# Queries and keys in 96 partitions of six tokens, and the order of the first loads, in a fused attention and expert kernel

## The chip, the cores and the metric

The kernel runs on one core of a Trainium2 chip. The metric is the device time of one execution in microseconds (us); of several executions, the median. The engines are TensorE (PE, with its weight loads as PEld), VectorE (DVE), ScalarE (ACT), GpSimd (POOL) and SyncE (SP), which issues most transfers. A transfer issued from SP, ScalarE or GpSimd stands in that engine's queue; an issue that waits holds up whatever is behind it.

## The reference

Causal attention for 4 batches of 8 heads, 576 tokens, head size 64, with a bias from running sums of a score per token, then a routed expert layer and a last feed-forward layer. Of it the change touches the attention:

```
scores = scale * q @ k.T                      # (4, 8, 576, 576)
cum = cumsum(maximum(s, 0))                   # s: (4, 8, 576)
bias = -(cum[:, :, :, None] - cum[:, :, None, :])
scores = where(causal, -1e9, scores + minimum(bias, 0))
attn = exp(scores - max(scores)); attn = attn / sum(attn)
out = attn @ v
```

## The kernel before, in words

The heads go in 8 groups g of four, each group in two pairs pr of heads. A float32 operand is held as two parts, a high one rounded to float32r and a low remainder, and products are summed over the parts. The order of work is written out in steps t: a prologue from t = -16 (PRE = 16), then 224 blocks of scores from t = 0, seven for each of 32 heads. At each step `todo[t]` runs first, then one block (`emit_s`, L943 on), then at most two jobs of a list sorted by due step (`run_job`). `later(n, ...)` puts work n steps on. So the order of instructions on each engine is fixed when the program is built.

Loading a pair of heads (`load_qk`, L700): queries and keys come as 128 tokens in partitions for four blocks of tokens, and the last 64 tokens in a transfer of their own. That makes 6 transfers for a pair, all on SP. `t_unit` (L802) transposes them on TensorE against an identity, so that a token becomes a column: 4 blocks of 128 for the queries, 4 for the keys, and 2 for the tails. ScalarE evicts the high part from PSUM (L821), VectorE subtracts for the low part (L826). `dup` (L837) copies or transfers the parts to the tiles QKA and QKB, from which the scores are made; for g = 0 and 1 a string of letters says which of the six moves goes to ScalarE (a), VectorE (v) or a transfer (d).

The bias goes in by extra rows of the score product. In QA (queries) and KA (keys) partitions 0 to 63 hold the head's values. Partitions 64 to 68 hold ones and bias rows: KA 64 and 65 hold the high and low part of the running sum, QA 66 and 67 the negated ones, QA 68 the negated row maximum; the rest are ones. The running sums are made once, at the start (L741 to L746): maximum, scan, high part, low part on VectorE, two negations on ScalarE, in four rows of `brow`. Group 0 takes its rows by four transfers on SP (L755 to L759); the other groups take theirs from a copy in DRAM, `b_dram` (L762, `bias_rows` L831).

`guard` (L886) makes the scores a first time to find each row's maximum; VectorE reduces them (L903) with a throwaway output `junk`. `m_row` (L913) transposes the maxima, and a transfer on SP (L927) places the negated maxima in QA 68. A block needs that transfer. `v_split` (L866) makes the high and low part of the values.

The constants of the start: `ident` on GpSimd, the rows of ones on VectorE and GpSimd (L730, for g = 1 at t = -9), `identb` as a VectorE copy of `ident` (L774), `band`, `tri` and others on GpSimd. The values of group 0 are loaded by SP from t = -8, the gate weights (`load_w`, L714) by SP at t = 6.

Of the kernel before, what the change touches and what calls it, by code (L numbers as in the profile page):

```python
# [8 lines left out]
F32 = mybir.dt.float32  # L9
# [19 lines left out]
def fb(ap):  # L29
    return ap.bitcast(F32)  # L30
# [136 lines left out]
def build(ctx, tc, q, k, v, s, w_gate, w1, w2, w_in, w_out, out, debug=None):  # L167
# [13 lines left out]

    b_dram = dram.tile([32, 4, S], F32, name="b_dram")
    K = {}
# [498 lines left out]
def attention(ctx, tc, const, cv, q, k, v, s, w_gate, ident, L, x_dram, b_dram, setup):  # L682
    nc = tc.nc
    NG = 2 * B
    NB, LAG, GLAG, PRE = 28, 5, 5, 16
    one = ctx.enter_context(tc.tile_pool(name="a_one", bufs=1))
# [4 lines left out]

    qkraw = [one.tile([128, 2, 5, 2, D], F32, name=f"qkraw{i}") for i in range(2)]
    vraw = one.tile([128, 5, 4, D], F32, name="vraw")
# [6 lines left out]
    def load_qk(g, pr, n):  # L700

        t, h, src = n % 2, n // 2, (q, k)[n % 2]
        h0 = 4 * (g % 2) + 2 * pr
        if h < 2:
            nc.sync.dma_start(out=qkraw[pr][:, t, 0:4, h],
                              in_=src[g // 2, h0 + h, 0:512].rearrange("(i p) d -> p i d", p=128))
        else:
            nc.sync.dma_start(out=qkraw[pr][:64, t, 4],
                              in_=src[g // 2, h0:h0 + 2, 512:S].rearrange("h p d -> p h d"))

# [15 lines left out]
    KB, QB = [x[:, :, :S] for x in QKB], [x[:, :, S:] for x in QKB]  # L726
    brow = QKB[1][:32].rearrange("p h c -> p (h c)")[:, :4 * S].rearrange("p (j c) -> p j c", j=4)

    def ones(i, engine, heads):
        engine.memset(fb(QKA[i])[64:69, heads], 1.0)  # L730

    def pads(i):
        nc.gpsimd.memset(fb(QA[i])[0:64, :, 0:64], 0.0)

    nc.vector.memset(spos, 0.0)
# [4 lines left out]
    pads(0)  # L740
    nc.vector.tensor_scalar(srow, srow, 0.0, 8.0, op0=OP.max, op1=OP.mult)  # L741
    nc.vector.tensor_tensor_scan(scan, srow, spos, 0.0, op0=OP.add, op1=OP.add)
    nc.vector.tensor_copy(brow[:, 2], scan)
    nc.scalar.activation(brow[:, 0], scan, AF.Copy, scale=-1.0)
    nc.vector.tensor_sub(brow[:, 3], scan, fb(brow)[:, 2])
    nc.scalar.activation(brow[:, 1], fb(brow)[:, 3], AF.Copy, scale=-1.0)  # L746

# [6 lines left out]

    for j in (2, 0, 3, 1):  # L755
        if j < 2:
            nc.sync.dma_start(out=fb(QA[0])[66 + j:67 + j, :, 64:], in_=fb(brow)[0:4, j])
        else:
            nc.sync.dma_start(out=fb(KA[0])[62 + j:63 + j], in_=fb(brow)[0:4, j])  # L759
    for n in range(6):  # L760
        load_qk(0, 1, n)
    nc.sync.dma_start(out=b_dram, in_=fb(brow))  # L762
    nc.gpsimd.memset(vraw[64:128, 4], 0.0)
# [4 lines left out]
    init_v(0)  # L768
    idwg = one.tile([128, 128 + 4 * E], F32, name="idwg")
    nc.gpsimd.tensor_copy(idwg[:, 16:144], ident)  # L770
    tiny = one.tile([128, 1], F32, name="tiny")
    nc.gpsimd.memset(tiny, 1e-9)
# [29 lines left out]
    def t_unit(g, pr, n):  # L802

        if n == 0:
            QK[g, pr] = rot.tile([128, 4, S], F32R, name="qk", bufs=2)
        st = QK[g, pr]
        p = bank()
        if n < 2:
            for r in range(4):
                nc.tensor.transpose(p[:, 128 * r:128 * r + 128], qkraw[pr][:, n, r], ident)  # L810
            src, hd = p, st[:, 1 + n, 0:512]
            los = [(src, hd, st[:, 3 * (1 - n), 0:512])]
        else:
            for t in range(2):
                nc.tensor.transpose(p[:, 128 * t:128 * t + 128], qkraw[pr][:, t, 4], ident)
            src = p[:, :256].rearrange("p (t c) -> p t c", t=2)[:, :, :64]
            hd = st[:, 1:3, 512:]
            los = [(src[:, t], st[:, 1 + t, 512:], st[:, 3 * (1 - t), 512:]) for t in range(2)]
# [12 lines left out]
    def bias_rows(g, pr):  # L831
        i, hs = g % 2, slice(2 * pr, 2 * pr + 2)
        rows = b_dram[4 * g + 2 * pr:4 * g + 2 * pr + 2].rearrange("h j t -> j h t")
        nc.sync.dma_start(out=fb(QA[i])[66:68, hs, 64:], in_=rows[0:2])
        nc.sync.dma_start(out=fb(KA[i])[64:66, hs], in_=rows[2:4])

    def dup(g, pr):  # L837
# [48 lines left out]
    def guard(g, pr, u):  # L886
# [186 lines left out]
    for g in range(NG):  # L1073
        s0 = NB * g
        for pr in range(2):
            b = s0 + 14 * pr
            for n in range(3):
                at = {0: -PRE + 9 * pr, 1: 4 + 6 * pr, 2: 16 + 6 * pr}.get(g, b - 52) + n
                job(at, max(at, b - 49 + 2 * n), t_unit, g, pr, n)
        pl = []  # L1080
        if g == 0:
            pl += [(8 - PRE + n // 2, load_v, (g, n)) for n in range(5)] + [(22 - PRE, load_w, ())]
        if g:
            for pr in range(2):
# [15 lines left out]
    while t < len(blocks) or queue or jobs or any(k >= t for k in todo):  # L1100
# [63 lines left out]
```

## Time and profile before

| | us |
|---|---|
| median of 3 runs | 1044.74 (1041.9 to 1045.15) |
| the profiled execution's own time | 1042.71 |
| its span, first to last instruction | 1041.0 |
| TensorE busy in the span | 956.0 (92%) |
| VectorE busy | 635.1 (61%) |
| ScalarE busy | 624.3 (60%) |
| GpSimd busy | 428.2 (41%) |

The times of instructions below count from the start of the span. Lines (L826) are those of the kernel before. The attention takes about the first 293 us of the span, the experts and the last layer the rest. The granted clock is a share of TensorE's full clock.

### The profile page before, as it was taken

The numbers are of one execution on the slowest core, as the hardware profiler recorded it, in microseconds if no ns is written. First come the engines' busy times: TensorE is split into PE (matmuls) and PEld (weight loads), VectorE is DVE, ScalarE is ACT, GpSimd is POOL, SyncE is SP. The second block draws the span as 40 slices with busy tenths as digits, with TensorE's granted clock in tenths as the row PEclk, the third lists the DMA queues.
The fourth block names the chain that finished last, engine by engine and source line by source line (L and its number), as shares of the span: only waits on it lengthen the run. The fifth ranks groups of instructions, "written<-read, shape, count | busy, mean of one in ns | idle before, by whom it ended". The sixth has DMA issues, their size and how long they took to land.

```text
span 1041.0 us, 21440 instructions
## 1 busy us (share of the span) xinstructions
PE 956.0 (92%) x7695; PEld 922.6 (89%) x7695; DVE 635.1 (61%) x1893; ACT 624.3 (60%) x1389; POOL 428.2 (41%) x425
## 2 busy tenths in 40 slices
PE   6979989999936779899999999999999999999996
PEld 5879878988836679899999999999999999999996
DVE  7667797798676668655545644644655564443243
ACT  4657776676842346645745664674674575675574
POOL 5446666467766632460342125036035123602401
PEclk8789998899966889999999999999999999999998
DMA  5799989895237433330321212123123022501200
GB/s 120 177 191 204 209 185 208 198 211 133 64 105 221 144 104 90 97 105 2 94 75 41 71 51 89 42 65 105 40 65 93 13 84 69 150 12 30 76 2 23
DMA packets 133298, 105.57 MB, mean 101 GB/s; under 512 B 63720, under 2 KB 114056, under 8 KB 133160
## 3 DMA queue, kind: packets, MB, share of 16 engines
q1 hardware_dynamic: 122520, 83.50, 32.6%
q10 hardware_dynamic: 7600, 11.27, 3.6%
q0 software_dynamic: 3072, 9.44, 2.9%
q8 instruction: 60, 0.98, 0.4%
q14 instruction: 46, 0.38, 0.1%
HBM read 69.55 MB, written 9.73 MB: 76 GB/s over the span
## 4 chain that ended last, share of the span: by engine, by line
PE 60%; DVE 14%; issue 10%; DMA 6%; ACT 5%; POOL 3%; SPq 1%; ACTq 0%; POOLq 0%; DVEq 0%
PE y L472 8%; PE y L474 8%; PE y L473 8%; PE hp L472 5%; PE hp L474 5%; PE hp L473 5%; PE words L472 3%; PE words L474 3%; PE words L473 2%; DMA QKB<-qk 2%; PE rt L260 2%; DVE mask L256 2%; DVE junk L903 1%; PE pv L1002 1%; PE pv L1004 1%
## 5 line engine op out<-in xcount | busy, mean ns | idle before, releaser
L442 POOL TENSOR_TENSOR wt<-raw,wt 128x512 fp32r<-128x512 f32 x112 | 142.8, 1293 | 167.4 <-ACT wt L441 161.5
L982 POOL TENSOR_TENSOR Pl<-P,Ph 128x384 fp32r<-128x384 f32 (+2 forms) x128 | 136.4, 1073 | 97.0 <-DVE Ph L981 43.9
L472 PE MATMUL y<-act,WO 128*128 128x288 f32 x516 | 156.4, 303 | 0.0
L473 PE MATMUL y<-act,WO 128*128 128x288 f32 x516 | 153.5, 297 | 0.2
L474 PE MATMUL y<-act,WO 128*128 128x288 f32 x516 | 153.6, 298 | 0.0
L472 PE MATMUL hp<-xu,WI 128*128 128x288 f32 x372 | 113.4, 305 | 6.7 <-DVE c L574 5.4
L474 PE MATMUL hp<-xu,WI 128*128 128x288 f32 x372 | 111.0, 298 | 0.0
L473 PE MATMUL hp<-xu,WI 128*128 128x288 f32 x372 | 110.0, 296 | 0.0
L473 PEld LDWEIGHTS y<-act,WO 128*128 128x128 f32 x516 | 98.2, 190 | 0.6 <-DVE act L580 0.6
L474 PEld LDWEIGHTS y<-act,WO 128*128 128x128 f32 x516 | 98.6, 191 | 0.0
L472 PEld LDWEIGHTS y<-act,WO 128*128 128x128 f32 x516 | 98.5, 191 | 0.0
L377 POOL DMA_INDIRECT xg<-x_dram,idx x24 | 22.5, 939 | 184.2 <-DVE rt L383 178.9
L441 ACT ACTIVATE wt<-raw 128x512 fp32r<-128x512 f32 x112 | 70.0, 625 | 40.7 <-DMA raw<-in_moe_w_dram 12.9
L974 ACT ACTIVATE P<-s 128x384 f32<-128x384 f32 (+2 forms) x128 | 63.7, 503 | 40.3 <-PE s L967 24.3
L566 ACT ACTIVATE c<-c 128x288 f32<-128x288 f32 x128 | 56.5, 441 | 45.6 <-DVE c L565 41.7
L574 DVE SCALAR_TENSOR_TENSOR hp<-c,hp 128x288 f32<-128x288 f32 x75 | 34.5, 460 | 76.3 <-ACT c L569 76.1
L472 PEld LDWEIGHTS hp<-xu,WI 128*128 128x128 f32 x372 | 70.8, 190 | 9.3 <-DVE c L574 7.2
L1002 PE MATMUL pv<-Ph,VH 128*128 128x320 f32 (+4 forms) x224 | 74.0, 330 | 4.5 <-DVE xT L1021 4.2
L965 PE MATMUL s<-QKB 128*128 128x320 f32 (+4 forms) x224 | 71.6, 320 | 0.0
L473 PEld LDWEIGHTS hp<-xu,WI 128*128 128x128 f32 x372 | 71.0, 191 | 0.3
L474 PEld LDWEIGHTS hp<-xu,WI 128*128 128x128 f32 x372 | 70.9, 190 | 0.0
L1004 PE MATMUL pv<-Pl,VH 128*128 128x320 f32 (+4 forms) x224 | 68.2, 304 | 1.4 <-POOL Pl L982 1.3
(274 smaller groups left out, 2991.9 us busy)
## 6 DMA issues: line engine op xcount, KB each, us to landing
raw<-in_moe_w_dram SPq DMA_DIRECT2D x120, 256.0 KB
QKB<-qk SPq DMA_DIRECT2D x55, 288.0 KB
QKA<-qk SPq DMA_DIRECT2D x29, 288.0 KB
qkraw<-in_q_dram SPq DMA_DIRECT2D x32, 128.0 KB
qkraw<-in_k_dram SPq DMA_DIRECT2D x32, 128.0 KB
vraw<-in_v_dram SPq DMA_DIRECT2D x32, 128.0 KB
x_dram<-xn SPq DMA_DIRECT2D x16, 256.0 KB
r<-in_moe_w_in_dram ACTq DMA_DIRECT2D x8, 512.0 KB
```

The costliest lines, as they stand in the source:

```text
L441: nc.scalar.activation(t[:, 0], r, AF.Copy)
L442: nc.gpsimd.tensor_sub(t[:, 1], r, fb(t)[:, 0])
L472: nc.tensor.matmul(out_ap, ah, bh, start=first, stop=False)
L473: nc.tensor.matmul(out_ap, ah, bl, start=False, stop=False)
L474: nc.tensor.matmul(out_ap, al, bh, start=False, stop=last)
L566: nc.scalar.activation(a, a, AF.Exp)
L574: nc.vector.scalar_tensor_tensor(u, a, 0.5, p[:, :CAP], op0=OP.subtract, op1=OP.mult)
L965: nc.tensor.matmul(p[:m, at:at + n], KB[i][:, h, kc], QB[i][:, h, q0:q1], start=ti in (1, 2) and j == 0, stop=False, skip_group_check=True)
L974: nc.scalar.activation(P[:, :n], p[:, :n], AF.Exp, scale=0.125)
L982: nc.gpsimd.tensor_sub(Pl[:, :n], P[:, :n], fb(Ph)[:, :n])
L1002: nc.tensor.matmul(o, VH[i][:, a, hs], ph, start=first, stop=False)
L1004: nc.tensor.matmul(o, VH[i][:, a, hs], pl, start=False, stop=last)
```

## The change

Queries and keys are loaded as 96 partitions of six consecutive tokens (NR = 6, NP = 96): one transfer for each head of each of the two, 4 for a pair. A transpose takes 96 tokens, every sixth one, so ScalarE's eviction and VectorE's subtraction write the columns at a step of six words. Units 0 and 1 of a pair do five residues of queries or keys, unit 2 the last residue of both.

The rows of the running sum are no longer negated. QA's ones become plain ones and KA's rows 66 and 67 become -1 (`signs`, made on ScalarE for g = 0 and GpSimd for g = 1), so `brow` and `b_dram` hold two rows in place of four. Group 0's rows go by SP for QA and by ScalarE's queue for KA, after the evictions at t = -13.

The first loads, for both pairs and for the values of group 0, stand at the head of SP. `identb` is built by GpSimd, the ones of the first group by VectorE, those of the second by GpSimd ahead of the steps, and the gate weights are loaded from GpSimd's queue. Some steps move: the duplication of the first pair, its guards and the maximum of its second head, loads of groups 1 and 2, and the V splits of groups 0 and 1. `junk` has one buffer instead of two.

```diff
-    qkraw = [one.tile([128, 2, 5, 2, D], F32, name=f"qkraw{i}") for i in range(2)]
+    qkraw = [one.tile([128, 2, NR, 2, D], F32, name=f"qkraw{i}") for i in range(2)]
...
-        t, h, src = n % 2, n // 2, (q, k)[n % 2]
-        h0 = 4 * (g % 2) + 2 * pr
-        if h < 2:
-            nc.sync.dma_start(out=qkraw[pr][:, t, 0:4, h],
-                              in_=src[g // 2, h0 + h, 0:512].rearrange("(i p) d -> p i d", p=128))
-        else:
-            nc.sync.dma_start(out=qkraw[pr][:64, t, 4],
-                              in_=src[g // 2, h0:h0 + 2, 512:S].rearrange("h p d -> p h d"))
+        t, h = n % 2, n // 2
+        nc.sync.dma_start(out=qkraw[pr][:NP, t, :, h],
+                          in_=(q, k)[t][g // 2, 4 * (g % 2) + 2 * pr + h].rearrange("(p r) d -> p r d", r=NR))
...
-            nc.sync.dma_start(out=idwg[:, 144 * x:144 * x + 16].rearrange("p (c e) -> p c e", c=2),
+            nc.gpsimd.dma_start(out=idwg[:, 144 * x:144 * x + 16].rearrange("p (c e) -> p c e", c=2),
...
-    for n in range(6):
-        load_qk(0, 0, n)
+    for pr in range(2):
+        for n in range(4):
+            load_qk(0, pr, n)
+    for n in range(5):
+        load_v(0, n)
...
+    sign = one.tile([128, 1], F32, name="sign")
+    nc.gpsimd.memset(sign, 1.0)
+    for past, value in ((66, -1.0), (68, 1.0)):
+        nc.gpsimd.affine_select(out=sign, in_=sign, pattern=[[1, 1]], compare_op=OP.is_ge, fill=value,
+                                base=past - 1, channel_multiplier=-1)
+    signs = sign[64:69, :, None].to_broadcast([5, 4, S])
...
-    for i in range(2):
-        nc.vector.memset(qkraw[i][64:128, :, 4], 0.0)
-    ones(0, nc.vector, slice(0, 2))
-    ones(0, nc.gpsimd, slice(2, 4))
...
-    nc.scalar.activation(brow[:, 0], scan, AF.Copy, scale=-1.0)
-    nc.scalar.activation(brow[:, 1], fb(brow)[:, 3], AF.Copy, scale=-1.0)
...
+    nc.vector.memset(fb(QA[0])[64:69], 1.0)
+    nc.scalar.activation(KA[0][64:69], signs, AF.Copy)
...
-    nc.vector.tensor_copy(identb, ident)
+    nc.gpsimd.memset(identb, 0.0)
+    nc.gpsimd.affine_select(out=identb, in_=identb, pattern=[[-1, 128]], compare_op=OP.not_equal,
+                            fill=1.0, base=0, channel_multiplier=1)
...
+    load_w()
+    init_v(1)
+    pads(1)
+    nc.gpsimd.memset(fb(QA[1])[64:69], 1.0)
+    nc.gpsimd.tensor_copy(KA[1][64:69], signs)
...
+    def first_rows(queue, x):
+        for j in range(2):
+            r = (66, 64)[x] + j
+            queue.dma_start(out=(fb(QA[0])[r:r + 1, :, 64:], fb(KA[0])[r:r + 1])[x], in_=fb(brow)[0:4, j])
+
+    first_rows(nc.sync, 0)
...
+        tokens = st.rearrange("p t (j r) -> p t r j", r=NR)
...
-            for r in range(4):
-                nc.tensor.transpose(p[:, 128 * r:128 * r + 128], qkraw[pr][:, n, r], ident)
+            for r in range(NR - 1):
+                nc.tensor.transpose(p[:, NP * r:NP * r + NP], qkraw[pr][:NP, n, r], ident[:NP, :NP])
+            src = p[:, :S - NP].rearrange("p (r j) -> p r j", r=NR - 1)
+            hd = tokens[:, 1 + n, 0:NR - 1]
+            los = [(src, hd, tokens[:, 3 * (1 - n), 0:NR - 1])]
...
-            later((1, 4)[pr] if g == 0 else 0, low)
+            later((3, 4)[pr] if g == 0 else 0, low)
...
-            later(max(2, NB * g + 14 * pr - 41 - now[0]) if g or pr == 0 else 2, dup, g, pr)
+            later(max(2, NB * g + 14 * pr - 41 - now[0]) if g else 1 + pr, dup, g, pr)
...
-            at = u + 2 if g == 0 and pr else now[0] + {0: 1, 1: 5}.get(g, 8) + u
+            at = now[0] + {1: 5}.get(g, 8) + u
+            if g == 0:
+                at = u + 2 if pr else u + (5 if u < 4 else 7) - PRE
...
-                junk = rot.tile([128, 512], BF16, name="junk")
+                junk = rot.tile([128, 512], BF16, name="junk", bufs=1)
...
-            job(now[0] + 2, now[0] + 2, m_row, g, pr, u // 4)
+            at = 2 if (pr, u) == (0, 7) else now[0] + 2
+            job(at, at, m_row, g, pr, u // 4)
...
-                at = {0: -PRE + 9 * pr, 1: 4 + 6 * pr, 2: 16 + 6 * pr}.get(g, b - 52) + n
+                at = {0: -PRE + 10 * pr, 1: 4 + 6 * pr, 2: 16 + 6 * pr}.get(g, b - 52) + n
...
-        if g == 0:
-            pl += [(8 - PRE + n // 2, load_v, (g, n)) for n in range(5)] + [(22 - PRE, load_w, ())]
...
-                at = {1: -12 + 9 * pr, 2: 8 + 6 * pr}.get(g, s0 + 14 * pr - 64)
-                pl += [(at + (2 * n if g > 2 else n), load_qk, (g, pr, n)) for n in range(6)]
-            pl += [(max(s0 - 44, 23) + 2 * n if g > 1 else 2 * n + 6, load_v, (g, n)) for n in range(5)]
+                at = {1: -12 + 9 * pr, 2: 9 + 6 * pr}.get(g, s0 + 14 * pr - 62)
+                pl += [(at + n, load_qk, (g, pr, n)) for n in range(4)]
+            pl += [(max(s0 - 44, 20) + 2 * n if g > 1 else 2 * n + 1, load_v, (g, n)) for n in range(5)]
+        at = (-3, 16)[g] if g < 2 else s0 - 20
...
-        if t == 7 - PRE:
-            ones(1, nc.gpsimd, slice(0, 4))
-            pads(1)
-            init_v(1)
+        if t == 3 - PRE:
+            first_rows(nc.scalar, 1)
```

## Rows read from the trace of the kernel before

**Rows 1.** Stretches: length, each engine's busy us (instructions), granted clock, DMA share, GB/s.

```profile
0.00:24.30 24.30, 14.99 (x109) 13.10 (x109) 19.89 (x45) 10.92 (x14) 12.90 (x21) 0.86 0.52 115
...
125.00:200.00 75.00, 68.95 (x467) 63.29 (x465) 58.71 (x197) 49.57 (x111) 43.97 (x47) 0.89 0.96 204
200.00:250.00 50.00, 48.19 (x357) 43.59 (x356) 46.03 (x154) 37.07 (x85) 34.80 (x32) 1.00 0.82 189
...
27.90:41.60 13.70, 13.70 (x60) 12.96 (x61) 8.33 (x31) 5.99 (x14) 6.51 (x7) 0.50 0.79 179
```

**Rows 2.** Timeline of the first leg: start us, us, engine, line, operation, tiles.

```profile
7.85 4.14 POOL L730 MEMSET QKA<- 5x4864 f32 x1
8.35 3.72 DVE L774 CAST identb<-ident 128x128 bf16<-128x128 f32 x1
9.05 1.20 ACT L821 ACTIVATE qk<-t 128x512 fp32r<-128x512 f32 x3
10.00 0.57 SPq L757 DMA_DIRECT2D QKA<-QKB  x1
12.78 0.55 PE L897 MATMUL s<-QKA 68*128 68x64 f32 x2 [2.17 <-DVE QKA L853]
```

**Rows 3.** Timeline of the second and third leg.

```profile
19.68 0.28 DVE L923 TENSOR_SCALAR mt<-pv 5x128 fp32r<-5x128 f32 x1 [0.74 <-PE pv L919]
22.45 0.79 SPq L927 DMA_DIRECT2D QKA<-mt  x1
24.31 1.36 ACT L876 ACTIVATE VH<-vraw 128x640 fp32r<-128x640 f32 x2 [1.72 <-DMA vraw<-in_v_dram]
24.33 0.39 PE L967 MATMUL s<-QKA 69*128 69x256 f32 x1 [0.20 <-DMA QKA<-mt]
25.58 0.47 ACT L974 ACTIVATE P<-s 128x384 f32<-128x384 f32 x1
```

**Rows 4.** The chain that ended last: start us, us, what.

```profile
44.80 3.42 DMA QKB<-qk
...
57.59 4.87 DMA QKB<-qk
```

**Rows 5.** Timeline of SP's queue, 0 to 65 us: second, a middle and the last.

```profile
1.30 0.41 SPq L705 DMA_DIRECT2D qkraw<-in_q_dram  x1
...
30.34 2.02 SPq L716 DMA_DIRECT2D idwg<-in_moe_w_gate_dram  x2
...
64.65 0.43 SPq L698 DMA_DIRECT2D vraw<-in_v_dram  x1
```

**Rows 6.** Groups by line on GpSimd: busy us, mean ns, idle before.

```profile
L377 POOL DMA_INDIRECT xg<-x_dram,idx x24 | 22.5, 939 | 184.2 <-DVE rt L383 178.9 <-issue 4.9 <-DVE rt L385 0.2
```

**Rows 7.** Waits of TensorE, 24 to 293 us: total us, times, longest.

```profile
PE t L815 <- DMA qkraw<-in_k_dram: 3.5, 4, 1.4
```

**Rows 8.** A chain row of four transposes, and two timeline rows of 64-column matmuls.

```profile
90.74 0.44 PE t L810 x4
...
45.40 0.27 PE L1003 MATMUL pv<-Ph,VL 128*128 128x64 f32 x1
45.51 0.28 PE L1004 MATMUL pv<-Pl,VH 128*128 128x64 f32 x1
```

**Rows 9.** Groups by line and form on ScalarE and VectorE: busy us, mean ns.

```profile
L821 ACT ACTIVATE qk<-t 128x512 fp32r<-128x512 f32 x32 | 18.9, 595 | 11.0 <-DMA QKB<-qk 5.4 <-PE t L810 3.7 <-PE s L897 1.5
L821 ACT ACTIVATE qk<-t 128x128 fp32r<-128x128 f32 x16 | 4.5, 282 | 1.3 <-PE t L815 1.2
...
L826 DVE TENSOR_TENSOR qk<-t,qk 128x512 fp32r<-128x512 f32 x32 | 23.0, 777 | 10.0 <-ACT qk L821 9.4
L826 DVE TENSOR_TENSOR qk<-t,qk 128x64 fp32r<-128x64 f32 x32 | 5.6, 215 | 4.1 <-ACT qk L821 4.0
...
L309 DVE TENSOR_REDUCE rt<-rt 128x8 f32<-128x144 f32 x8 | 2.4, 306 | 0.2 <-PE rt L306 0.2
...
L250 DVE TENSOR_REDUCE rt<-L 128x18 f32<-128x144 f32 x8 | 2.4, 300 | 0.0
```

More of the change, by code (lines that the diff above doesn't have):

```diff
@@ L180, in build @@
     x_dram = dram.tile([N, DM], F32, name="x_dram")
-    b_dram = dram.tile([32, 4, S], F32, name="b_dram")
+    b_dram = dram.tile([32, 2, S], F32, name="b_dram")
     K = {}
@@ L684, in attention @@
     NG = 2 * B
-    NB, LAG, GLAG, PRE = 28, 5, 5, 16
+    NB, LAG, GLAG, PRE, NR = 28, 5, 5, 16, 6
+    NP = S // NR
     one = ctx.enter_context(tc.tile_pool(name="a_one", bufs=1))
@@ L726, in attention @@
     KB, QB = [x[:, :, :S] for x in QKB], [x[:, :, S:] for x in QKB]
-    brow = QKB[1][:32].rearrange("p h c -> p (h c)")[:, :4 * S].rearrange("p (j c) -> p j c", j=4)
-    def ones(i, engine, heads):
-        engine.memset(fb(QKA[i])[64:69, heads], 1.0)
+    brow = QKB[1][:32].rearrange("p h c -> p (h c)")[:, :2 * S].rearrange("p (j c) -> p j c", j=2)
+    sign = one.tile([128, 1], F32, name="sign")
[4 more added lines that the diff above has]
+    signs = sign[64:69, :, None].to_broadcast([5, 4, S])
     def pads(i):
         nc.gpsimd.memset(fb(QA[i])[0:64, :, 0:64], 0.0)
-    nc.vector.memset(spos, 0.0)
-    for i in range(2):
-        nc.vector.memset(qkraw[i][64:128, :, 4], 0.0)
-    ones(0, nc.vector, slice(0, 2))
-    ones(0, nc.gpsimd, slice(2, 4))
[L740 to L743, printed above, removed]
-    nc.scalar.activation(brow[:, 0], scan, AF.Copy, scale=-1.0)
-    nc.vector.tensor_sub(brow[:, 3], scan, fb(brow)[:, 2])
-    nc.scalar.activation(brow[:, 1], fb(brow)[:, 3], AF.Copy, scale=-1.0)
     VH = [one.tile([128, 10, 192], F32R, name=f"VH{i}") for i in range(2)]
@@ L753, in init_v @@
         nc.gpsimd.memset(VL[i][:, :, 64:128].bitcast(F32), 0.0)
[L755 to L763, printed above, removed]
+    nc.vector.memset(spos, 0.0)
+    nc.vector.memset(fb(QA[0])[64:69], 1.0)
+    nc.scalar.activation(KA[0][64:69], signs, AF.Copy)
     band = one.tile([128, S], F32, name="band")
@@ L767, in attention @@
                             fill=-1e10, base=448, channel_multiplier=1)
[L768 to L772, printed above, removed]
+    pads(0)
     identb = one.tile([128, 128], BF16, name="identb")
-    nc.vector.tensor_copy(identb, ident)
+    nc.gpsimd.memset(identb, 0.0)
+    nc.gpsimd.affine_select(out=identb, in_=identb, pattern=[[-1, 128]], compare_op=OP.not_equal,
+                            fill=1.0, base=0, channel_multiplier=1)
     tri = one.tile([128, 128], BF16, name="tri")
@@ L778, in attention @@
                             fill=-1e10, base=0, channel_multiplier=-1)
+    tiny = one.tile([128, 1], F32, name="tiny")
+    nc.gpsimd.memset(tiny, 1e-9)
+    nc.gpsimd.memset(vraw[64:128, 4], 0.0)
+    init_v(0)
+    idwg = one.tile([128, 128 + 4 * E], F32, name="idwg")
+    nc.gpsimd.tensor_copy(idwg[:, 16:144], ident)
+    load_w()
[3 more added lines that the diff above has]
+    nc.gpsimd.tensor_copy(KA[1][64:69], signs)
+    nc.vector.tensor_scalar(srow, srow, 0.0, 8.0, op0=OP.max, op1=OP.mult)
+    nc.vector.tensor_tensor_scan(scan, srow, spos, 0.0, op0=OP.add, op1=OP.add)
+    nc.vector.tensor_copy(brow[:, 0], scan)
+    nc.vector.tensor_sub(brow[:, 1], scan, fb(brow)[:, 0])
+    def first_rows(queue, x):
[3 more added lines that the diff above has]
+    first_rows(nc.sync, 0)
+    nc.sync.dma_start(out=b_dram, in_=fb(brow))
     QK, MX = {}, {}
@@ L806, in t_unit @@
         st = QK[g, pr]
+        tokens = st.rearrange("p t (j r) -> p t r j", r=NR)
         p = bank()
         if n < 2:
-            for r in range(4):
-                nc.tensor.transpose(p[:, 128 * r:128 * r + 128], qkraw[pr][:, n, r], ident)
-            src, hd = p, st[:, 1 + n, 0:512]
-            los = [(src, hd, st[:, 3 * (1 - n), 0:512])]
+            for r in range(NR - 1):
[3 more added lines that the diff above has]
+            los = [(src, hd, tokens[:, 3 * (1 - n), 0:NR - 1])]
         else:
             for t in range(2):
[L815 to L818, printed above, removed]
+                nc.tensor.transpose(p[:, NP * t:NP * t + NP], qkraw[pr][:NP, t, NR - 1], ident[:NP, :NP])
+            src = p[:, :2 * NP].rearrange("p (t j) -> p t j", t=2)
+            hd = tokens[:, 1:3, NR - 1]
+            los = [(src[:, t], tokens[:, 1 + t, NR - 1], tokens[:, 3 * (1 - t), NR - 1]) for t in range(2)]
         def evac():
             nc.scalar.activation(hd, src, AF.Copy)
-            later((1, 4)[pr] if g == 0 else 0, low)
+            later((3, 4)[pr] if g == 0 else 0, low)
         def low():
@@ L833, in bias_rows @@
         rows = b_dram[4 * g + 2 * pr:4 * g + 2 * pr + 2].rearrange("h j t -> j h t")
-        nc.sync.dma_start(out=fb(QA[i])[66:68, hs, 64:], in_=rows[0:2])
-        nc.sync.dma_start(out=fb(KA[i])[64:66, hs], in_=rows[2:4])
+        nc.sync.dma_start(out=fb(QA[i])[66:68, hs, 64:], in_=rows)
+        nc.sync.dma_start(out=fb(KA[i])[64:66, hs], in_=rows)
     def dup(g, pr):
@@ L1077, in attention @@
             for n in range(3):
-                at = {0: -PRE + 9 * pr, 1: 4 + 6 * pr, 2: 16 + 6 * pr}.get(g, b - 52) + n
+                at = {0: -PRE + 10 * pr, 1: 4 + 6 * pr, 2: 16 + 6 * pr}.get(g, b - 52) + n
                 job(at, max(at, b - 49 + 2 * n), t_unit, g, pr, n)
         pl = []
-        if g == 0:
-            pl += [(8 - PRE + n // 2, load_v, (g, n)) for n in range(5)] + [(22 - PRE, load_w, ())]
         if g:
             for pr in range(2):
-                at = {1: -12 + 9 * pr, 2: 8 + 6 * pr}.get(g, s0 + 14 * pr - 64)
-                pl += [(at + (2 * n if g > 2 else n), load_qk, (g, pr, n)) for n in range(6)]
-            pl += [(max(s0 - 44, 23) + 2 * n if g > 1 else 2 * n + 6, load_v, (g, n)) for n in range(5)]
-        pl += [(s0 - 20 if g > 1 else 20 if g else 15 - PRE, v_split, (g, 0)), (s0 - 19 if g > 1 else 20 + 1 if g else 15 + 1 - PRE, v_split, (g, 1))]
+                at = {1: -12 + 9 * pr, 2: 9 + 6 * pr}.get(g, s0 + 14 * pr - 62)
+                pl += [(at + n, load_qk, (g, pr, n)) for n in range(4)]
+            pl += [(max(s0 - 44, 20) + 2 * n if g > 1 else 2 * n + 1, load_v, (g, n)) for n in range(5)]
+        at = (-3, 16)[g] if g < 2 else s0 - 20
+        pl += [(at + part, v_split, (g, part)) for part in range(2)]
         for st, fn, args in pl:
```

## The prediction, made before the changed kernel was run

> **What bounds the kernel now.** I read the busy times by stretch first, then the timeline and the chain of waits of the stretches in which TensorE is not full, then who waits for whom. In the stretch 125 to 200 us TensorE is busy 68.95 of 75 us and in 200 to 250 us 48.19 of 50, with VectorE at 46.03 [rows 1]: the steady attention is bound by TensorE, VectorE close behind. The start is not: in the first 24.3 us TensorE is busy 14.99 us, and that with warm-up matmuls. After the attention the change touches nothing, so what is won or lost before 293 us is the result.
>
> The start is a chain of three legs. First, the token sums. VectorE's copy of the 128x128 identity takes 3.72 us from 8.35 us, under a GpSimd memset of 5x4864 elements that runs from 7.85 us for 4.14 us and ends within 0.1 us of it; the first bound matmul starts at 12.78 us, released by the copies queued behind that cast [rows 2]. ScalarE's first eviction of a transpose starts at 9.05 us, behind two ScalarE negations of the token sums; the last of the four row transfers is issued at 10.00 us. Second, the maxima: the row of negated maxima is in SBUF at 19.96 us (19.68 + 0.28) but its transfer is issued at 22.45 us, behind loads on SP, and the first block's bias matmul starts at 24.33 us, released by that transfer [rows 3]. Third, ScalarE: its first exponential starts at 25.58 us. Later, two transfers of the duplicated keys stand in the chain with 3.42 us at 44.80 and 4.87 us at 57.59 us [rows 4], and SP issues 87 transfers in the first 65 us, 55.4 us in sum (the second, a middle one and the last in [rows 5]). SP is the queue that sets the early pace.
>
> **The change part by part.** *Token sums and constants, first leg.* The identity copy leaves VectorE (3.72 us); two negations leave ScalarE ahead of the first eviction (at 9.05 us); the memset of the one-rows goes to VectorE (5x2560 elements; at 4.14/4864 us each, 2.2 us, before the sums) and the row signs to ScalarE (2,304 elements; at the 0.815 ns worked out below, 2.1 us, between the table load and the first transposes, so hidden by the wait for loads). But the first bound matmul also needs the rows. Thirteen loads now stand ahead of them on SP; between the 0.41 us of the second issue and the mean of 0.64, about 0.55 each from 1.30 us [rows 5], SP reaches them at about 8.4 and has issued the second at about 9.6. In the kernel before, at most 2.78 us lie between the issue of the last row and the first bound matmul (10.00 to 12.78 us), so the matmul can start at 11 to 12 us. I take 11.5: 1.3 us won here. ScalarE issues the other two rows behind its evictions, two issues of about 0.6 us, ahead of copies that wait for VectorE anyway. If the wait for the token sums came late there, those copies and with them the first exponential would be late by as much. The price of this leg lies between 0 (the loads delay the rows by as much as the cast did) and 3.7 us (the cast).
>
> *Second and third leg.* With the subtractions done before the first bound scores, VectorE reduces as the scores come; half of the first pair's maxima move behind the first blocks; the transfer of the maxima finds SP free, which wins the 2.5 us between 19.96 and 22.45. The value loads now stand near the head of SP, so the V split (1.36 us on ScalarE from 24.31 us, which waited 1.72 us for its load [rows 3]) is done before the first exponential. Together 5 us for the three legs, 2 at least (the SP delay alone), 7 at most (the cast, the SP delay and the V split less overlap).
>
> *SP.* Each head pair needs 4 loads for 6: in the first 65 us 39 issues of queries and keys become about 26; the two gate loads (2.02 us [rows 5]) go to GpSimd's queue and two row issues to ScalarE's. At 0.64 us each (55.4/87) that is 8.3 + 2.0 + 1.3 = 11.6 us of 55.4. The stretches of 3.42 and 4.87 us begin with an issue on this queue and the second pair's and the value loads are moved into the first 10 us, so their transfers find a shorter queue. I take half of the 8.3 us, 4; the ends are 0 (the engines behind the queue are as busy as before, the bytes being the same) and 8.3.
> On GpSimd the two gate loads cost about 0.94 us each by the only GpSimd-issued transfers of the trace [rows 6], before its first V split; the memsets moved ahead fill time in which it is idle. The single junk buffer costs nothing: only VectorE writes it, in order; with a second engine there it would cost a wait per reduction.
>
> *Tail loads.* TensorE waits 3.5 us in four places for the transposes of the last 64 tokens [rows 7]. They have no transfers of their own after the change; the last residue comes with the loads the first transposes wait for. I take 1.5 us, between 0 (the wait moves to the first transposes) and 3.5.
>
> *Transposes.* 10 of 128 columns become 12 of 96 for each of 16 pairs. Four take 0.44 us, 0.11 each [rows 8]. If the columns set this, 12 x 0.083 = 0.99 us, 0.11 less than now; if the weight load does, 12 x 0.11 = 1.32, 0.22 more. The nearest row is a 64-column matmul with a full weight load: start to start 0.11 us (45.40 to 45.51) [rows 8]. So I take 0.22 x 16 = 3.5 us, of which 2.5 where TensorE is full; the ends are -1.8 and 3.5.
>
> *Evictions at a step of six words.* ScalarE's 512 elements take 595 ns and its 128 take 282, so 0.815 ns each; VectorE's 777 and 215 for 512 and 64, so 1.25 ns each [rows 9]. Per pair 1,152 elements stream through each, before and after. That ScalarE writes, and VectorE reads and writes SBUF, at a step of 24 bytes is not in the trace; the nearest row is a reduction that reads 144 elements at a step of 32 bytes from PSUM, 306 ns against 300 for contiguous ones [rows 9]. I take 0 from it. The other end is double: 0.94 us more on ScalarE and 1.44 on VectorE a pair.
> The Trainium skill, page "SBUF — State Buffer", section "Specifications (TRN2)", says that SBUF works in lines of 16 bytes and wants at least two hits in a line for full bandwidth. At a step of 24 bytes no line is hit twice; by that the other end would hold, and the sum would be that of the first rival. No run here shows such a step in SBUF.
>
> The sum against the profiled execution's 1042.7 us: -5 - 4 - 1.5 + 2.5 = -8, so 1034.7. The median of the three runs stands 2.0 us above that execution, so I say **1036.7**. About 0.3%, 3 us, is what a measurement of this kernel tells from no change.
>
> **The rivals.** *Strided evictions make VectorE the bound* (slower). Its place is the stretch from 125 to 250 us, where VectorE is busy 58.71 of 75 and 46.03 of 50 us [rows 1]. Price: 1.44 x 16 = 23 us of VectorE time. If all of it showed, 1037 + 23 = 1060; it decides when more than 12 us, half of it, cannot be hidden. For it: VectorE has only 4 us left of the 50. Against: the PSUM row, and the 16 us of slack in the stretch before. If only the pairs of the second half show, half the price (12) less the 4 us left, 1037 + 8 = 1045, no measurable change. Chance of slower 0.12. The page named above would put it higher.
>
> *The start is won, the queue is not* (no change). If the two stalls return elsewhere because the same bytes pass the same engines, -5 + 2.5 remains, some 2.5 us: 1044.7 - 2.5 = 1042. For it: the transfers' share is 0.96 in 125 to 200 us [rows 1]. Against: the 44.80 stall begins with an SP issue. With the half-hidden strides above, chance 0.18.
>
> *The clock follows* (faster still). TensorE holds the lower level from 27.9 to 41.6 us, granted 0.50 and busy all 13.7 us [rows 1]; work done there at the higher level would take half, so up to 6.9 us return if the denser start keeps the clock up: 1030. That level is 1.2 GHz of the two, 1.2 and 2.4. The reverse, another such stretch, would cost as much. Chance of the gain 0.2.
>
> **How the numbers follow.** Forecast 0.5, faster clock 0.2, no change 0.18, slower 0.12. So faster 0.70, same 0.18, slower 0.12. The forecast's own range is 1031 to 1041.5 (stalls and start towards their ends). To leave out no more than 2 in 10 the range goes down to 1025 (clock and both stalls) and up to 1047 (no change with half-hidden strides).
>
> **What would show it.** Right: the first exponential at 20 to 21 us, no VectorE cast of the identity, the maxima's transfer issued within 1 us of its row, about 70 SP issues in 65 us, no 3 us wait for a key transfer before 65 us, four transposes at 0.08 to 0.11 us each. ScalarE's 480-element eviction near 570 ns and VectorE's subtraction near 0.7 us say that the step costs nothing; 0.95 and 1.2 us or more say the first rival. Wrong: a first exponential after 24 us, since then the rows behind thirteen loads set the start; or equal stalls at 40 to 65 us; or VectorE above 48 of 50 us in 200 to 250 us with TensorE waiting for it.

## The result, and the profile after

The changed kernel takes 1054.63 us (median, 1052.31 to 1065.08) beside 1043.32 us of the kernel before: ratio 1.0126, 95% interval 1.0093 to 1.016. It is slower by about 11 us, outside the range, and the outcome is that of the first rival. The rows below are of the execution that took 1052.31 us (span 1050.6).

Groups by line and shape, changed kernel (busy us, mean ns of one, then idle time before it):

```profile
L834 DVE TENSOR_TENSOR qk<-t,qk 128x480 fp32r<-128x480 f32 x32 | 33.8, 1058 | 9.7 <-ACT qk L829 8.4 <-DMA vraw<-in_v_dram 1.0
L829 ACT ACTIVATE qk<-t 128x480 fp32r<-128x480 f32 x32 | 33.6, 1063 | 7.5 <-PE t L817 6.8 <-DMA r<-in_moe_w_out_dram 0.3
...
L834 DVE TENSOR_TENSOR qk<-t,qk 128x96 fp32r<-128x96 f32 x32 | 9.0, 329 | 1.7 <-ACT qk L829 1.4
L829 ACT ACTIVATE qk<-t 128x192 fp32r<-128x192 f32 x16 | 8.5, 530 | 0.0
```

These answer to [rows 9]. ScalarE needs 1063 ns for 480 elements where 512 took 595; VectorE 1058 ns where 512 took 777.

The start of the changed kernel in the timeline (start us, us; the bracket is idle time and what ended it). First the bound scores, then the maxima's transfer, then ScalarE up to the first exponential:

```profile
9.53 3.89 DVE L861 CAST QKA<-qk 64x1152 fp32r<-64x1152 f32 x2 [1.99 <-ACT qk L829]
...
10.06 2.75 POOL L770 MEMSET QKA<- 5x2560 f32 x1
10.11 1.50 SPq L781 DMA_DIRECT2D QKA<-QKB  x2
12.85 2.53 POOL L771 CAST QKA<-sign 5x2304 fp32r<-5x2304 f32 x1
...
14.31 0.56 PE L907 MATMUL s<-QKA 68*128 68x64 f32 x2 [2.88 <-DMA QKA<-QKB]
...
19.76 0.79 SPq L938 DMA_DIRECT2D QKA<-mt  x1
...
20.47 1.94 ACT L829 ACTIVATE qk<-t 128x480 fp32r<-128x480 f32 x2
22.43 1.37 ACT L886 ACTIVATE VH<-vraw 128x640 fp32r<-128x640 f32 x2
23.71 0.50 ACT L829 ACTIVATE qk<-t 128x192 fp32r<-128x192 f32 x1
24.24 1.17 ACT L859 ACTIVATE QKA<-qk 64x1152 fp32r<-64x1152 f32 x1
25.31 0.47 ACT L985 ACTIVATE P<-s 128x384 f32<-128x384 f32 x1
```

Against [rows 2, 3] the identity copy is gone and the maxima leave SP at 19.76 us, but the first bound matmul is 1.5 us later (14.31 for 12.78) and the first exponential 0.27 us earlier (25.31 for 25.58).

Where the time went, by the start of the first exponential (us) of some heads, one profiled execution each; the last column is the start of the last one. The kernels below "changed" are experiments, described further on; their executions took 1042.31 (e3), 1042.65 (e4), 1043.15 (e6), 1046.15 (e7), 1044.28 (e8), 1046.53 (e9), 1041.89 (e11) and 1050.25 us (e12).

| kernel | head 0 | head 2 | head 4 | last |
|---|---|---|---|---|
| before | 25.58 | 46.53 | 72.98 | 286.34 |
| changed | 25.31 | 48.67 | 74.85 | 297.31 |
| runs of five (e3) | 25.45 | 43.47 | 70.70 | 285.48 |
| old layout (e4) | 24.73 | 43.02 | 71.13 | 286.51 |
| runs, memset later (e6) | 24.20 | 45.27 | 70.88 | 287.60 |
| runs, rows first (e7) | 23.59 | 44.89 | 72.13 | 286.79 |
| runs, both edits (e8) | 26.02 | 42.82 | 72.54 | 287.04 |
| e8 without warm-ups (e9) | 24.26 | 46.79 | 74.10 | 289.01 |
| before, without warm-ups (e11) | 25.09 | 43.20 | 72.32 | 286.23 |
| e8 with a late start (e12) | 29.12 | 50.50 | 77.86 | 292.80 |

The loss is in the attention, where the last exponential starts 297.31 - 286.34 = 11 us later (the two executions differ by 9.6); it is not in the start and grows along the heads.

### The profile page after: what moved, and what is told of

It is laid out like the page before. It is cut to its first block, busy times and chain, and to the rows that moved or that the text cites. A ratio compares the mean times of both kernels' runs of the same rounds, so it can differ in the third digit from the quotient of the medians.

```text
span 1050.6 us, 21474 instructions
## 1 busy us (share of the span) xinstructions
PE 966.7 (92%) x7727; PEld 929.4 (88%) x7727; DVE 651.6 (62%) x1890; ACT 642.9 (61%) x1388; POOL 429.6 (41%) x432
## 4 chain that ended last, share of the span: by engine, by line
PE 47%; issue 6%; DVE 3%; ACT 1%; DMA 1%; POOL 1%; POOLq 0%; ACTq 0%
PE y L472 8%; PE y L474 7%; PE y L473 7%; PE hp L472 5%; PE hp L474 4%; PE hp L473 4%; PE words L472 3%; PE words L474 3%; PE words L473 2%; PE rt L260 1%; DVE mask L256 1%; PE hp L506 0%; PE rt L356 0%; PE hp L635 0%; DMA xg<-x_dram,idx 0%
## 5 line engine op out<-in xcount | busy, mean ns | idle before, releaser
L472 PEld LDWEIGHTS hp<-xu,WI 128*128 128x128 f32 x372 | 70.2, 189 | 9.9 <-DVE c L574 7.8
L473 PEld LDWEIGHTS hp<-xu,WI 128*128 128x128 f32 x372 | 70.3, 189 | 0.1
L474 PEld LDWEIGHTS hp<-xu,WI 128*128 128x128 f32 x372 | 70.0, 188 | 0.0
```

The source lines that it names most:

```text
L472: nc.tensor.matmul(out_ap, ah, bh, start=first, stop=False)
L473: nc.tensor.matmul(out_ap, ah, bl, start=False, stop=False)
L474: nc.tensor.matmul(out_ap, al, bh, start=False, stop=last)
```

## The experiments

**Is it the step of six words?** One kernel puts the residues side by side, so that the evictions write contiguously (its tokens come in another order, so it computes scores of permuted tokens). One keeps the token order and turns the walk: PSUM is read at a step of 96 words, SBUF written in runs of five of six. One has all of the change but the layout, one the layout alone.

```diff
 # contiguous                      (e1)
-        tokens = st.rearrange("p t (j r) -> p t r j", r=NR)
+        tokens = st.rearrange("p t (r j) -> p t r j", r=NR)
 # runs of five                    (e3)
-        tokens = st.rearrange("p t (j r) -> p t r j", r=NR)
+        tokens = st.rearrange("p t (j r) -> p t j r", r=NR)
...
-            src = p[:, :S - NP].rearrange("p (r j) -> p r j", r=NR - 1)
-            hd = tokens[:, 1 + n, 0:NR - 1]
+            src = p[:, :S - NP].rearrange("p (r j) -> p j r", r=NR - 1)
+            hd = tokens[:, 1 + n, :, 0:NR - 1]
...
```

The contiguous one, the runs, the old layout in the changed kernel, the new layout in the kernel before:

> The changed kernel with the evictions and subtractions of the transposes writing contiguously (the residues side by side, so the tokens of a head stand in another order and the scores belong to permuted tokens; the work is the same). If the step of six words is the cause (theory S), ScalarE's 480 elements fall from 1063 to about 570 ns, VectorE's from 1058 to about 700 ns, and the time falls by 10 us or more, to 1044 or below. If the late rows of the start and VectorE's wait for GpSimd are the cause (theory P), the durations fall but the time stays at 1050 or above. If the clock alone is (theory C), the time stays within 3 us of the changed kernel's and the durations do not matter.

> The changed kernel with the same columns in the same places, but the eviction walks token by token: it reads PSUM at a step of 96 words and writes runs of five words in six. Theory S with the step on the SBUF side: ScalarE's 480 elements take about 570 to 700 ns, VectorE's 700 to 900, the time falls to 1040 to 1046. If the step costs on the PSUM side as well, the durations stay near 1060 ns and the time near 1054. Theory P: durations fall, time stays at 1050 or above.

> All of the change but the layout: two bias rows with sign rows, first loads at the head of SP, constants on other queues, the new steps, with the old loads of 128 tokens (six transfers a pair) and the old transposes. Theory S: the rest of the change is worth 0 to -5 us, so 1038 to 1044. Theory P: the start is what costs, so the time is 1048 or more, as the first bound matmul still starts at 14 us or later.

> The kernel before with the new layout alone (96 partitions of six tokens, four transfers a pair, evictions at a step of six words, one junk buffer), all else as before. Theory S: 1052 to 1060, most of the loss or more. Theory P: within 3 us of the kernel before, as the start is the old one.

Measured: contiguous 1045.22 us, ratio to the kernel before 1.0017 (0.9989 to 1.0044); runs 1045.11, 1.0016 (0.9998 to 1.0033); old layout 1045.65, 1.0023 (1.0001 to 1.0044); layout alone 1058.46, 1.0128 (1.0084 to 1.0173). The groups of the kernel with contiguous writes:

```profile
L834 DVE TENSOR_TENSOR qk<-t,qk 128x480 fp32r<-128x480 f32 x32 | 20.8, 653 | 4.9 <-ACT qk L829 3.9 <-DMA vraw<-in_v_dram 0.5
L829 ACT ACTIVATE qk<-t 128x480 fp32r<-128x480 f32 x32 | 18.3, 571 | 10.1 <-PE t L817 9.4 <-DMA r<-in_moe_w_out_dram 0.3
L834 DVE TENSOR_TENSOR qk<-t,qk 128x96 fp32r<-128x96 f32 x32 | 6.6, 247 | 3.4 <-ACT qk L829 3.4
L829 ACT ACTIVATE qk<-t 128x192 fp32r<-128x192 f32 x16 | 5.4, 337 | 0.0
```

and of the one with runs of five, whose last residue is still written at a step of six:

```profile
L834 DVE TENSOR_TENSOR qk<-t,qk 128x480 fp32r<-128x480 f32 x32 | 20.8, 653 | 4.1 <-ACT qk L829 3.6
L829 ACT ACTIVATE qk<-t 128x480 fp32r<-128x480 f32 x32 | 18.4, 574 | 9.5 <-PE t L817 6.5 <-DVE mx L913 1.8 <-DMA r<-in_moe_w_out_dram 0.6
L834 DVE TENSOR_TENSOR qk<-t,qk 128x96 fp32r<-128x96 f32 x32 | 9.0, 328 | 3.4 <-ACT qk L829 3.2
L829 ACT ACTIVATE qk<-t 128x192 fp32r<-128x192 f32 x16 | 8.6, 535 | 0.0
```

The step alone turns 571 ns into 1063 and 653 into 1058. Reading PSUM at a step of 96 words costs nothing (574 and 653). The layout without the rest gives the full slowdown and more (15 us over the 1043.25 us of the kernel before that ran with it); take the step away and 9.5 us go (1054.63 - 1045.11), known to some us only, since the changed kernel's four executions span 13 us. The step is the cause, theory S; theories that lay the loss on the start or on the clock alone fall, since the kernels with runs and with contiguous writes have the changed start too. But the rest of the change, which the prediction put at -8, is worth nothing that was measured.

**Where the price begins.** A block ahead of the attention runs 480-element instructions by themselves at output steps of 1, 2, 3, 4, 6 and 8 words, then VectorE's with its output, its SBUF input, or both at such steps.

```diff
+    for s in (1, 2, 3, 4, 6, 8):
+        nc.scalar.activation(at(wide, s), p[:, :N], AF.Copy)
...
+    for s in (1, 2, 3, 4, 6, 8):
+        nc.vector.tensor_sub(at(wid2, s), p[:, :N], fb(wide)[:, :N])
+    for s in (1, 2, 3, 4, 6, 8):
+        nc.vector.tensor_sub(wid2[:, :N], p[:, :N], at(fb(wide), s))
+    for s in (1, 6):
+        nc.vector.tensor_sub(at(wid2, s), p[:, :N], at(fb(wide), s))
```

> The kernel before with a block in front of the attention that times 480-element instructions by themselves at output and input steps of 1, 2, 3, 4, 6 and 8 words; the whole time is not the point (some 30 to 40 us more). Theory S (SBUF pays for each line that it touches, and a step of six words touches a new line with each word): ScalarE's write takes about 570 ns at steps 1 and 2 and about 1060 ns from 4 on, 3 between; VectorE's subtraction about 650 ns with both contiguous, about 1050 ns with the output at step 6, and the same if only its SBUF input is at step 6 when reads pay as writes do. Rival W (only writes pay): the subtraction with the strided input stays at about 650 ns. Rival R (the cost grows with the step, in bytes spanned): each step dearer than the one before, 8 dearer than 6, and 2 already over 570 ns. Reading PSUM turned and writing runs of five: as contiguous by S.

Its timeline: ScalarE at the six output steps; VectorE with its output at a step of six (L188); with its input at steps of two, three and four (L190); with both at six (L192):

```profile
9.59 0.57 ACT L182 ACTIVATE wide<-pprobe 128x480 fp32r<-128x480 f32 x1 [7.48 <-DVE wide L177]
10.19 0.59 ACT L182 ACTIVATE wide<-pprobe 128x480 fp32r<-128x480 f32 x1
10.82 0.80 ACT L182 ACTIVATE wide<-pprobe 128x480 fp32r<-128x480 f32 x1
11.65 1.01 ACT L182 ACTIVATE wide<-pprobe 128x480 fp32r<-128x480 f32 x1
12.70 1.00 ACT L182 ACTIVATE wide<-pprobe 128x480 fp32r<-128x480 f32 x1
13.73 1.03 ACT L182 ACTIVATE wide<-pprobe 128x480 fp32r<-128x480 f32 x1
...
19.24 1.00 DVE L188 TENSOR_TENSOR wid<-pprobe,wide 128x480 fp32r<-128x480 f32 x1
...
22.02 0.66 DVE L190 TENSOR_TENSOR wid<-pprobe,wide 128x480 fp32r<-128x480 f32 x1
22.71 0.78 DVE L190 TENSOR_TENSOR wid<-pprobe,wide 128x480 fp32r<-128x480 f32 x1
23.53 0.99 DVE L190 TENSOR_TENSOR wid<-pprobe,wide 128x480 fp32r<-128x480 f32 x1
...
27.32 0.99 DVE L192 TENSOR_TENSOR wid<-pprobe,wide 128x480 fp32r<-128x480 f32 x1
```

On ScalarE a step of two is free (0.59 us), three takes 0.80, four 1.0 us, and six and eight are no dearer: rival R falls. A strided read costs VectorE as much as a strided write (0.99 and 1.00 us), so W falls; both together (the last row) cost no more than one. The whole kernel took 1073.13 us in one execution, the block included.

**What became of the start.** Two edits on the kernel with runs of five, alone and together: the second buffer's memset and sign rows put later in the program, and group 0's two rows issued on SP ahead of the value loads.

```diff
 # memset later                    (e6)
-    nc.gpsimd.memset(fb(QA[1])[64:69], 1.0)
-    nc.gpsimd.tensor_copy(KA[1][64:69], signs)
...
+        if t == 7 - PRE:
+            nc.gpsimd.memset(fb(QA[1])[64:69], 1.0)
+            nc.gpsimd.tensor_copy(KA[1][64:69], signs)
 # rows first                      (e7)
-    for n in range(5):
-        load_v(0, n)
...
     first_rows(nc.sync, 0)
+    for n in range(5):
+        load_v(0, n)
```

> The changed kernel with the eviction in runs of five, and GpSimd's memset and sign rows of the second buffer (with its pads and V constants) back at their old later place. Theory H (VectorE's two bias copies are held under GpSimd's memset of 5x2560 elements, 3.9 us for two where ScalarE's or a free VectorE's would take about 1.3): the two copies take about 1.4 us, the first bound matmul starts 2 us earlier, at 12 us, the first exponential at 23 to 24 us and the time is 1 to 2 us under that of the kernel with runs (1045.1). Rival R (the bias rows behind thirteen loads set the start): the first bound matmul stays at 14 us, released by the rows, and the time is the same within 1 us. Rival C (the clock gives back what the start wins): first exponential earlier, time unchanged.

> The changed kernel with the eviction in runs of five, and the two bias rows of the first group issued on SP ahead of the five value loads. Theory H (the held copies set the start): first bound matmul stays at 14 us, first exponential at 25 us, time within 1 us of 1045.1. Rival R (the rows behind the loads set it): first bound matmul about 2 us earlier, time 1 to 2 us less. The value loads land 3 to 4 us later, which costs nothing as long as the V split stays before the first exponential at 25 us.

> Both edits together: memset and sign rows of the second buffer later, bias rows ahead of the value loads. Theories H and R together (each a leg of the start, the later one hides the other): first bound matmul at 11 to 12 us, the 11.5 that the prediction gave, first exponential at 21 to 23 us, and 3 to 4 us less than 1045.1 if what the start wins is kept: about 1041.5, below the kernel before. Rival C (the clock: the denser start meets its low stretch earlier or longer and gives the win back by head 4): first exponential as early, head 4 and the time within 1 us of the kernel with runs alone, 1044 to 1046.

Measured: memset later 1044.93 us, 1.0019 (1.0001 to 1.0037); rows first 1046.22, 1.0013 (0.9986 to 1.004); both 1044.28, 1.0014 (0.9991 to 1.0037). The first edit tested nothing of theory H: GpSimd, idle, reached the memset at 8.52 us instead of 10.06, so VectorE's two copies still ran beside it (9.49 us, 4.44 long). The second brought the first bound matmul from 14.14 (runs of five) to 13.25 us and the first exponential to 23.59. With both the matmul starts at 12.62, yet the first exponential at 26.02. So the rows set the bound matmul in part (rival R), and VectorE's two copies do not (theory H): the matmul starts before the second copy ends, at 13.25 against 13.34 (9.34 + 4.00) and at 12.62 against 14.01 (9.29 + 4.72).

The rest of the way to the first exponential goes with TensorE's clock; this is read from the traces and was not tested by itself. TensorE has the second pair's transposes and bounds and the warm-ups to do ahead of the first block. Busy times by stretch (PE, PEld, DVE, ACT, POOL, then clock) with runs of five, then with rows first:

```profile
15.00:25.00 10.00, 10.00 (x66) 8.75 (x66) 6.47 (x28) 8.64 (x10) 3.34 (x3) 0.50 0.44 98
19.70:23.60 3.90, 3.73 (x37) 2.86 (x35) 3.03 (x12) 3.84 (x7) 2.01 (x2) 1.00 0.32 73
```

Four warm-ups, with rows first and with both edits:

```profile
20.71 0.40 PE L1104 MATMUL pv<-ident 128*128 128x128 bf16 x4
...
21.04 0.65 PE L1100 MATMUL pv<-ident 128*128 128x128 bf16 x4
```

With runs of five TensorE works at 0.50 and ScalarE, free by then, waits 1.66 us for its scores; with rows first it works at 1.00. With both edits the trace has no record of the clock before 26.6 us, but the warm-ups take 0.65 us and not 0.40, as they do with runs of five. No version started the exponentials before 23.59 us, and none gained time.

The kernel with both edits was 3.7 us ahead of the kernel before at head 2 and had 0.4 left at head 4. Busy time by stretch, TensorE alone (length, busy us and count, granted clock, transfers' share), kernel before:

```profile
44.00:66.00 22.00, 15.18 (x102) 0.91 0.92 190
63.00:69.70 6.70, 5.77 (x25) 0.56 1.21 213
```

and the kernel with both edits:

```profile
27.90:41.60 13.70, 12.45 (x99) 1.00 1.08 199
44.00:66.00 22.00, 20.49 (x91) 0.50 1.16 177
```

Where the kernel before held the lower level, 27.9 to 41.6 us [rows 1], this one has the full clock; from 44 to 66 us, where the kernel before waited for transfers at 0.91, it is busy 20.49 of 22 us at 0.50, the lower of the two levels (1.2 of 2.4 GHz), and does 91 matmuls for 102. TensorE's idle time fell from 6.8 to 1.5 us, and half clock came in its place. By busy time times clock it did 10.2 us of full-clock work there for 13.8, an estimate whose difference of 3.6 us is about the 3.3 us lost by head 4.

**Does TensorE's earlier work decide that, and does a late start cost?** Without the four warm-up matmuls per step, in this kernel and in the one before; and with eight ScalarE copies ahead of the first exponential.

```diff
-        if 4 - PRE <= t < 0 and 4:
-            warm(4)
 # late start
+        if t == 0:
+            late = rot.tile([128, 512], F32, name="P", bufs=3)
+            for _ in range(8):
+                nc.scalar.activation(late[:, :480], band[:, :480], AF.Copy)
```

> The kernel with both start edits and the eviction in runs, without the four warm-up matmuls per step ahead of the first block (the 25 in one go stay). Theory C (the clock gives back what the start wins: in the kernel with both edits it was granted in full until 44 us and then at 0.50 from 44 to 66 us, TensorE busy 20.5 of those 22 us, where the kernel before held 0.50 from 27.9 to 41.6 and about 0.56 from 63 to 69.7): with TensorE less busy in the first 25 us the low stretch comes later or is shorter, or moves into the warm-up time; head 4 starts 2 us or more before the 72.5 us of the kernel with both edits and the time is under 1043. Rival T (the first blocks need the warm-up: a cold TensorE does the first bound scores and blocks at the lower level): first exponential 1 to 3 us later than 26.0 and the time 1 to 3 us more. Rival N (the low stretch is set by the attention's own work from 25 us on): head 4 and the time within 1 us.

> The kernel before without the four warm-up matmuls per step ahead of the first block, the control of the run above. Theory C: as there, less low clock before 70 us, head 4 earlier than 72.98 us. Rival T: the time 1 to 3 us more. Rival N: within 1 us.

> The kernel with both start edits and the eviction in runs, with eight ScalarE copies of 128x480 elements (8 x 0.57 = 4.6 us) put ahead of its first exponential, so that the start is made later on purpose. Theory C (what the start wins or loses is gone by head 4, because TensorE's low stretch and the work of the first heads take it up): first exponential 3 to 4.6 us later, head 4 within 1.5 us of 72.5 and the time within 1.5 us of the kernel with both edits (1044.3). Rival E (a later start is a later end; only a gain gets lost): head 4 and the time 3 to 4.6 us later, about 1048.

Measured: both edits without warm-ups 1045.53 us, 1.0014 (0.9995 to 1.0033); before without warm-ups 1042.31, 0.9993 (0.9975 to 1.001); late start 1049.33, 1.0047 (1.0027 to 1.0066). Without warm-ups nothing changed that can be measured, in either kernel: the ratio of the one is 1.0014 with and without, the other is about 1 us less, inside its interval. For the time theory N is nearest, although heads 2 and 4 of the first come 4.0 and 1.6 us later. The late start of the third:

```profile
24.18 5.04 ACT L1114 ACTIVATE P<-band 128x480 f32<-128x480 f32 x8
29.12 0.47 ACT L981 ACTIVATE P<-s 128x384 f32<-128x384 f32 x1
```

Its first exponential is 3.1 us later than without the copies, head 4 5.3 and the median 5.0 (by the ratios, 1.0047 and 1.0014, 3.4): rival E. A late start is paid in full; theory C, that the first heads take up whatever the start does, falls in this form. What is shown is that no variant kept a gain to the end that can be measured: the runs of five, 2.3 us ahead of the kernel before at head 4, are 0.9 ahead at the last exponential.

**Four and two residues in place of five and one**, so that no word is written singly:

> The kernel with both start edits, its six residues taken as four and two instead of five and one, so that the eviction writes runs of four and of two of six words and none single. Theory S: ScalarE's eviction of 384 elements takes about 490 ns in both forms (572 ns for 480, less 96 at 0.815) and VectorE's subtractions of 384 and 192 about 550 and 330 ns; a pair costs ScalarE 1.47 us (1.68 with five and one) and VectorE about 1.75 (1.96). Time within 1 us of the kernel with both edits (1044.3), since neither engine is the bound there; more than 1.5 us less would say that VectorE still costs.

Measured: 1044.89 us, 1.0014 (0.9992 to 1.0035); ScalarE 517 ns for 384 elements, VectorE 553 and 349. The eviction is no longer what decides. No version of the changed kernel beat the kernel before.

## Why the prediction was wrong

*Evictions at a step of six words*, the failed step: "I take 0 from it". The nearest row was a VectorE reduction that reads PSUM at a step, which the runs of five found to be free; the new accesses write, and VectorE's read, SBUF, of which that row says nothing. Against contiguous writes of the same shapes a pair's evictions cost ScalarE 2 x (1063 - 571) + (530 - 337) = 1.18 us and VectorE 2 x (1058 - 653) + 2 x (329 - 247) = 0.97 us more; the other end had been 0.94 and 1.44. Its 1.25 ns an element of VectorE was too high: the mean of 777 ns holds two subtractions of the start that read 2.43 and 1.82 us behind the identity cast, and the other 30 take 687. The Trainium skill, page "SBUF — State Buffer", section "Specifications (TRN2)", asks for two hits in a line of 16 bytes; the runs agree: ScalarE's 480 elements took 0.59 us at a step of 8 bytes and 1.01 at 16. The Trainium skill also had a price that I overlooked: page "Vector Engine (DVE) Microarchitecture Reference", section "5.2 Measured stream behaviour on trn2 (trn3 not measured)", puts an element that hops on one port at some 0.65 VectorE cycle more, and small steps higher than large ones. At its 1.04 ns a cycle that is 0.68 ns, an estimate. The rows give (0.99 - 0.66) / 480 = 0.7 ns, and no more than that at the small step of six words.

*The first rival* had the right cause and nearly the right size (it gave 1045 to 1060), but not quite the way: VectorE was not full. The stretches of the changed kernel (PE, PEld, DVE, ACT, POOL, then clock):

```profile
65.00:125.00 60.00, 56.92 (x406) 51.43 (x405) 48.06 (x161) 45.19 (x94) 35.41 (x32) 0.96 0.86 189
125.00:200.00 75.00, 69.06 (x460) 62.70 (x458) 62.52 (x198) 52.27 (x107) 43.22 (x47) 0.88 0.87 195
200.00:250.00 50.00, 47.19 (x344) 42.35 (x343) 43.86 (x140) 38.82 (x81) 28.45 (x26) 0.97 0.86 189
```

and with runs of five:

```profile
65.00:125.00 60.00, 58.52 (x446) 53.99 (x445) 47.52 (x172) 45.90 (x102) 37.82 (x35) 0.99 0.93 200
125.00:200.00 75.00, 70.11 (x474) 64.08 (x473) 61.07 (x199) 50.28 (x111) 43.95 (x48) 0.89 0.90 199
200.00:250.00 50.00, 46.84 (x342) 41.44 (x341) 45.32 (x149) 36.29 (x81) 34.07 (x31) 1.00 0.85 193
```

VectorE had 43.86 of 50 us, not over 48. In part it is lateness: TensorE waits for the subtraction that frees its bank. Waits from 65 to 285 us of the changed kernel (sum, times, longest):

```profile
PE t L1058 <- DVE qk L834: 3.2, 8, 0.6
```

The kernel with runs has no such wait there. In these 185 us TensorE is idle 11.8 us against 9.5, and granted less: missing clock times length is 2.4 + 9.0 + 1.5 = 12.9 us against 8.9. Together, as an estimate, 6.3 of the 7.7 us by which the changed kernel falls behind that with runs between head 4 (4.15 us) and head 26 (11.9). That the step makes the loss is shown; this path from it, by idle time and clock, is read from two executions, and why TensorE holds the lower level longer is open.

*The start, -5*: failed. The maxima's transfer did leave at once (19.76 us) and SP was no longer in the way, but two other things were late. The bound matmul came at 14.31, not 11.5: SP reached the rows at 10.11, not 8.4 (1.7 us of the error), and the matmul, released by a transfer of such rows, came 4.2 us after that and not 3.1 (1.1 us). VectorE did not become free either: its two copies, beside memsets of GpSimd as before, took 3.89 us (3.83 before), though the bound matmul did not wait for the second. And ScalarE, with the second pair's evictions moved ahead of the V split (1.94 + 1.37 + 0.50 + 1.17), reached its first exponential at 25.31, not 20 to 21. With runs of five ScalarE is done earlier and the exponential starts no sooner (25.45), since TensorE is at half clock; the leg of the clock was not in the sum. I had priced the work that left, not the work moved in ahead.

*SP, -4*: SP's issues in the first 65 us fell from 87 (55.4 us) to 71 (46.7), as said. With the old layout the stalls of [rows 4] stay (3.60 us at 42.95, 5.70 at 55.13 in its chain). With four loads a pair the chain of the kernel with runs has none between 38 and 72 us, but that with both edits has 6.42 us at 41.17 and 3.49 at 67.46. The gain of the kernel with both edits showed at head 2 and was gone by head 4, with half clock in between. The clock rival failed in the changed kernel, granted 0.50 from 27.9 to 41.6 us as before. With both edits it came true for that stretch (1.00), and the low level came back from 44 to 66: the low stretch moved. Whether a full clock from 44 to 66 us would have kept the gain can't be tried.

*Tail loads, -1.5*: the four waits went (3.5 us), but the first transposes wait 6.2 us for their loads where they waited 5.1, the end that the prediction named; no run prices it alone. *Transposes, +2.5*: too high, and by the trace of the wrong sign; five of 96 columns take 0.58 us in the timeline where four of 128 took 0.60. From start to start they are 86 ns apart in the median where they were 113, about as 96 to 128, so the columns set it here, and a pair's twelve cost no more than ten did.

So of the 11.3 us between the medians the step makes 9.5, and the rest of the change, put at -8, makes 1.8 (1045.11 - 1043.32), near what a measurement can tell from nothing.

## What to carry to other kernels

When a change leaves the instruction count alone but alters the step of an access, price it by a row that touches the same memory at the same step; if there is none, neither "the nearest row" nor zero is safe. Where a transpose leaves columns at a stride, try to turn the walk so that the step falls on the PSUM side and SBUF is written in runs: a few lines, some 9.5 us here. And at a start, list for each engine what is moved in ahead of the first block, not only what leaves.

## What the runs showed of the hardware

ScalarE and VectorE keep their rate at a step of two words in SBUF (0.59 and 0.66 us for 480 elements), pay in full at four (1.01 and 0.99) and no more at six (1.00 and 0.99); reads and writes at a step don't add up. PSUM read at a step of 96 words runs at the contiguous rate (574 for 571 ns, 653 for 653).

VectorE's copy of 64x1152 elements takes 0.76 us where no GpSimd instruction runs (at 45.59 us of the changed kernel). Started beside a GpSimd memset it ended 0.61 us after that one, on five partitions as on 128: at 13.42 after a memset on five that ends at 12.81, and in the kernel before at 14.68 after one on 128 that ends at 14.07.

And in one stretch of 22 us, 44 to 66, TensorE either waited for transfers at a granted 0.91 (kernel before) or worked on at 0.50 (both edits), and head 4 began within 0.5 us of the same time.
